# The gate weights as the stationary operand for four transposed tiles at once, and the put-off batches' columns cut into four parts

## The chip, the core and the metric

The program runs on one core of a Trainium2 chip. The metric is the time of one execution on the device in microseconds (us). The kernel before takes 1412.26 us (median of 3 runs, 1411.99 to 1412.28).

TensorE is PE in the profile (PEld is its weight load), VectorE is DVE, ScalarE is ACT, GpSimd is POOL, and SyncE, which issues most DMAs, is SP. A matmul has a stationary operand (the weights, loaded first) and a moving operand whose columns stream past it.

## The reference

Three stages follow each other, all in float32. Two attention steps give x, one row of 512 for each of 4608 tokens (8 batches of 576). A dense layer pair with a leaky ReLU follows: 512 to 2048 to 512. Then each token goes to one of 8 experts, which are chosen by the largest remaining of all logits, with at most 576 tokens for an expert.

```python
p_packed = sm_attn(p, k, v)
out = sm_attn(q, p_packed, p_packed)       # -> x [4608, 512]
h = x @ w_in
g = np.maximum(0.01 * h, h)
x2 = g @ w_out                             # [4608, 512]
logits = x2 @ w_gate                       # [4608, 8]
order = np.argsort(-logits.flatten())      # greedy assignment, capacity 576
...
out[mask] = np.maximum(x2[mask] @ w1[e], 0.0) @ w2[e]
```

The gate product x2 @ w_gate has only 8 columns. It is kept in float32, since the order of the logits decides the routing.

## The kernel before

**Stages.** `packs` computes the packed keys and values and folds the first dense layer into them (0 to about 125 us of the trace). `tokens` goes through batches 0 to 5 in 16 units each (128 of the 2048 hidden columns are one unit): `mm1` (L917) makes the hidden rows of the unit in two halves of 288 tokens, ACT and DVE evacuate and split them into a high and a low float32r part (L927, L928, L939, L942), and the second layer (`mm2_list`, L1082) adds 12 or 15 matmuls per unit to the batch's sums, one unit later. Batches 6 and 7 are put off: their first layer is done as side units inside batches 4 and 5 (`SIDE`, `side_unit`), split and stored to DRAM (`put`, L1011), and their second layer fills the PE's waits in the routing stage (`PutOff`), for which `get` (L1018) loads the stored parts again. Then come the routing (a serial chain of 12 steps on DVE and PE), and the experts.

**Where the logits come from.** For batches 0 to 4 the finished rows are multiplied by w_gate. `evac` (L1023) copies each 128-row tile out of PSUM and queues two pieces with `times_gate` (L1056): `turn` transposes the tile in four 128x128 blocks (L1065) and ACT copies them to SBUF (L1067); `product` (L1069) multiplies them by the gate weights, with the transposed block (128x128) as the stationary and the 8 gate columns as the moving operand (L1072), and DVE copies 128x8 to the logits L (L1073). For batches 5 to 7 the rows are not ready in time, so the kernel multiplies w_out by w_gate first (`wog_pieces`, the same two pieces for each of 16 tiles of w_out, whose high and low parts POOL adds at L953) and takes the logits from the hidden rows: `logits` (L961) has the 32 columns of `wog` of one unit as stationary operand and the unit's tokens as moving operand, in four column groups of the array (outputs on PSUM partitions 0, 32, 64 and 96). The 512 main tokens are four parts of 128 (L979); the 64 tail tokens go behind the fourth part (L980), and in batch 5 the tail tokens of batch 4 behind the first (L983). DVE adds the parts to `lg` (L986), and `logits_of` (L990) transposes `lg` back after the last unit (L996, L997).

**What sets the order.** On PE the order of batches 1 to 5 is written out in `tokens`: before each unit up to `XS` = 3 pieces are taken, those of the next batch's queries first, then gate pieces from `tk.dots` and, where room is left, from `gates` (the w_out pieces). They are emitted one at a time between the parts of the unit by `small()`. The functions of a piece without `pe` (the POOL addition) go with the piece in front. On all other engines, on PE in batch 0, and in the last four side units after batch 5, a scheduler orders the instructions by its own timeline. The PSUM bank of the pieces is `x`, with one buffer, or `acc5` in even batches.

A float32 matmul that isn't a transpose appears in the trace as two records, a transpose as one: the 38 products of four matmuls are 304 records of L1072, and the 48 units of `logits` are 384 records of L979.

Of the kernel before, what the change touches and what calls it, by code (L numbers as in the profile page):

```python
# [6 lines left out]
F32 = mybir.dt.float32  # L7
# [9 lines left out]
B, H, S, DH, NP_ = 8, 8, 576, 64, 32  # L17
D, FF = 512, 2048
E, F2, CAP = 8, 1024, 576
# [9 lines left out]
class Lag:  # L29


    def __init__(self):
        self.q = []
# [29 lines left out]
def pe(fn):  # L63

    def piece():
        return fn()
    piece.pe = True
    return piece
# [14 lines left out]
def f32(ap):  # L83
    return ap.bitcast(F32)
# [421 lines left out]
QE, XS = 14, 3  # L506
# [10 lines left out]
ND = 2  # L517
# [261 lines left out]
class Tokens:  # L779
# [165 lines left out]
    def wog_pieces(self):  # L945

        nc = self.nc
        st = {}

        def whole(f):  # L950
            t = self.two.tile([128, D], F32, name="wsum", tag="raw64")
            st[f] = t
            nc.gpsimd.tensor_add(t, f32(self.wo(f, 0)), f32(self.wo(f, 1)))  # L953

        fns = []
        for f in range(self.NF):
            turn, product = self.times_gate(lambda f=f: st[f], lambda f=f: self.wog[:, f, :E])
            fns += [lambda f=f: whole(f), turn, product]
        return fns

    def logits(self, b, f, tf):  # L961

        nc, PE = self.nc, self.nc.tensor
        both = b == B - ND - 1
        if f == 0:
            if b < B - ND:
                t = self.P.two.tile([128, 192], F32, name="lg2", tag="at2")  # L970
            else:
                t = self.one.tile([128, 192], F32, name="lg")
            nc.gpsimd.memset(t, 0.0)
            self.lg[b] = t
        lg = self.lg[b]
        ps = self.bank([128, 192])
        w = self.wog[:, f]
# [12 lines left out]
    def logits_of(self, b):  # L990
        nc = self.nc
        V, PE = nc.vector, nc.tensor
        c0, c8 = 9 * (b // 2) + 4 * (b % 2), 9 * (b // 2) + 8
        lt = self.lg.pop(b)
        ps = self.P.ps.tile([128, 2, 4, 4 * E], F32, name="x")
        PE.transpose(ps[:, 0].rearrange("p q e -> p (q e)"), lt[:, :128], self.ident)  # L996
        PE.transpose(ps[:64, 1].rearrange("p q e -> p (q e)"), lt[:, 128:], self.ident)  # L997
        V.tensor_copy(self.L[:, c0:c0 + 4], ps[:, 0, :, :E])
        lo = (b % 2) * 64
        V.tensor_copy(self.L[lo:lo + 64, c8], ps[:64, 1, 3, :E])  # L1000
        if b == B - ND - 1:
            V.tensor_copy(self.L[:64, c8], ps[:64, 1, 0, :E])
        if b % 2:
            self.R.look(self.two, c0 - 4, c0 + 5)

# [17 lines left out]
    def evac(self, b, acc, gate=True):  # L1023

        nc, P = self.nc, self.P
        V, A = nc.vector, nc.scalar
        bp = b // 2
        for r in range(4):
# [3 lines left out]
            if gate:  # L1032
                self.gate(x, 9 * bp + 4 * (b % 2) + r)
        if b % 2:
            x = self.wk1.tile([128, D], F32, name="x2tail")
            A.copy(x, acc[4])
            for i in range(2):
                r0 = (b - 1 + i) * S + 512
                nc.sync.dma_start(self.x2d[r0:r0 + 64], x[64 * i:64 * i + 64])
            if gate:  # L1040
                self.gate(x, 9 * bp + 8)
                self.dots.add([lambda: self.R.look(self.two, 9 * bp, 9 * bp + 9)])

    def gate(self, x, col):

        self.dots.add(self.times_gate(lambda: x, lambda: self.L[:, col]))

    def bank(self, shape):

# [6 lines left out]
    def times_gate(self, rows, out):  # L1056

        nc, PE = self.nc, self.nc.tensor
        st = {}

        def turn():
            x = rows()
            ps = self.bank([128, 4, 128])
            for c in range(4):
                PE.transpose(ps[:, c], x[:, c * 128:(c + 1) * 128], self.ident)  # L1065
            st["t"] = self.two.tile([128, 4, 128], F32, name="rowt")
            nc.scalar.copy(st["t"], ps)  # L1067

        def product():  # L1069
            ps = self.bank([128, E])  # L1070
            for c in range(4):
                PE.matmul(ps, st["t"][:, c], self.wg[:, c], start=c == 0, stop=c == 3)  # L1072
            nc.vector.tensor_copy(out(), ps)  # L1073
        return [pe(turn), pe(product)]


def mm2_list(nc, acc, g, tl, wh, wl, start, stop):
# [343 lines left out]
def tokens(tk, pk, keep, first, st, acc_pools):  # L1421
# [43 lines left out]
    for b in range(B - ND):  # L1465
# [3 lines left out]
        for q in SIDE_Q[b]:  # L1469
            if q:  # L1470
                side_q(*q)
            elif b + 1 < B - ND:
                nat, fns = tk.q_side(b + 1)
                qs.add(fns)
        with ordered(tk.tc, b > 0):
            for f in range(NF):
# [3 lines left out]
                if f % 2 == 0:  # L1480
                    wcur = w
                    nb, nf = (b, f // 2 + 1) if f // 2 < 7 else (b + 1, 0)
                    if nb < B - ND:
# [4 lines left out]
                        w = tk.wp_load(nb, nf)  # L1488
                tk.spare = b > 0 and b % 2 == 0 and 2 <= f

                xs = must[:]
                must.clear()
                if b:
                    tabs.pop(1)
                    for x in (qs, tk.dots, gates):
# [3 lines left out]
                    for more in (tk.dots, gates):  # L1499
                        while len(xs) < XS:  # L1500
                            x = more.take()
                            if x is None:
                                break
                            xs.append(x)

                def small(n=1):
                    for _ in range(min(n, len(xs))):
# [2 lines left out]
                t = tk.mm1(at, wcur, slice((f % 2) * 128, (f % 2) * 128 + 128))  # L1510
# [129 lines left out]
```

## Time and profile before

| | |
|---|---|
| median of the runs | 1412.26 us |
| profiled execution: its own time | 1415.55 us |
| profiled execution: span of the core | 1413.8 us |
| PE busy | 1347.5 us, 95% of the span |
| PE weight load busy | 1126.1 us, 80% |
| DVE busy | 732.4 us, 52% |
| ACT busy | 559.5 us, 40% |
| POOL busy | 309.1 us, 22% |
| batches 1 to 5 with the side units | about 250 to 806 us |
| routing | about 830 to 960 us |

Busy time is the union of an engine's instructions. Matmuls are pipelined and overlap in the records, so what one costs is read from the start of one group to the start of the next, not from its duration. The time of the profiled execution is 3.3 us above the median, and its span 1.5 us.

### The profile page before, as it was taken

The page shows a single profiled execution, that of the slowest core. Times are in us where ns is not written, and L with a number is a line of the kernel's source. Part 1 is how long each engine was busy: PE and PEld are TensorE (multiplying, and loading weights), DVE is VectorE, ACT ScalarE, POOL GpSimd, SP SyncE. Part 2 cuts the span into 40 slices and gives each one's busy share as a digit, 9 for nine tenths or more (in the row PEclk, how much of TensorE's full clock was granted, in tenths as well). Part 3 has the DMA queues.
Part 4 walks back from the last instruction along what each step waited for, and adds up shares of the span by engine and source line. Part 5 has one row for each costly group of instructions (what it writes and reads, how often), then busy time and mean ns, then how long its engine had stood idle before and what let it go on. Part 6 is the DMA issues. An engine that isn't in the chain of part 4 may idle for free. (4 is left out here: it accounts for less than half of the span.)

```text
span 1413.8 us, 25670 instructions
## 1 busy us (share of the span) xinstructions
PE 1347.5 (95%) x10206; PEld 1126.1 (80%) x10206; DVE 732.4 (52%) x1878; ACT 559.5 (40%) x1209; POOL 309.1 (22%) x293
## 2 busy tenths in 40 slices
PE   7999898999999999999999988997999999999997
PEld 4667776888888888788788866776998998898896
DVE  4776898433354445666455566782344344344331
ACT  4765555544445345555444420003233233233231
POOL 3322234244222112322122110002121121121011
PEclk9999999999999999999999999997999999999999
DMA  9998565210212112333223464546243443442320
GB/s 267 305 300 259 183 193 167 84 32 20 85 41 75 51 40 77 126 111 107 103 97 110 139 211 136 158 129 220 94 134 102 137 135 93 146 134 77 117 76 38
DMA packets 147881, 180.49 MB, mean 128 GB/s; under 512 B 27952, under 2 KB 105776, under 8 KB 147760
## 3 DMA queue, kind: packets, MB, share of 16 engines
q1 hardware_dynamic: 122992, 141.08, 32.1%
q10 hardware_dynamic: 19008, 18.88, 4.6%
q0 software_dynamic: 5760, 18.88, 3.7%
q8 instruction: 81, 1.33, 0.4%
q14 instruction: 40, 0.33, 0.1%
HBM read 124.27 MB, written 54.53 MB: 126 GB/s over the span
## 5 line engine op out<-in xcount | busy, mean ns | idle before, releaser
L1082 PE MATMUL acc<-wout,g 128*128 128x512 f32 x1728 | 454.3, 407 | 15.3 <-ACT wout L803 5.7
L1082 PEld LDWEIGHTS acc<-wout,g 128*128 128x128 f32 x1728 | 315.0, 191 | 84.0 <-issue 7.5
L928 DVE SCALAR_TENSOR_TENSOR t<-t 128x576 f32<-128x576 f32 x128 | 105.1, 821 | 140.1 <-ACT t L927 139.7
L927 ACT COPY t<-h 128x288 f32<-128x288 f32 x256 | 100.9, 400 | 182.0 <-PE h L80 181.8
L78 PE MATMUL h<-xt,w1hl 128*128 128x288 f32 x504 | 149.1, 296 | 2.0 <-DVE eg__12337 L1216 2.0
L79 PE MATMUL h<-xt,w1hl 128*128 128x288 f32 x504 | 149.3, 296 | 0.0
L80 PE MATMUL h<-xt,w1hl 128*128 128x288 f32 x504 | 149.2, 296 | 0.0
L78 PE MATMUL h<-at,wphl 128*128 128x288 f32 x384 | 123.7, 322 | 0.6 <-ACT t L927 0.6
L79 PE MATMUL h<-at,wphl 128*128 128x288 f32 x384 | 114.0, 297 | 0.0
L80 PE MATMUL h<-at,wphl 128*128 128x288 f32 x384 | 113.7, 297 | 0.0
L905 POOL TENSOR_TENSOR wphl<-wpraw,wphl 128x512 fp32r<-128x512 f32 x48 | 68.2, 1420 | 190.2 <-ACT wphl L904 189.4
L942 DVE TENSOR_TENSOR g<-t,g 128x512 fp32r<-128x512 f32 (+1 forms) x96 | 80.8, 841 | 39.7 <-ACT g L939 39.4
L78 PEld LDWEIGHTS h<-xt,w1hl 128*128 128x128 f32 x504 | 95.3, 189 | 4.8 <-ACT w2hl L1107 2.4
L1158 POOL DMA_INDIRECT xg<-x2d,idx x36 | 34.6, 960 | 288.6 <-PE x L1181 148.6
L79 PEld LDWEIGHTS h<-xt,w1hl 128*128 128x128 f32 x504 | 95.3, 189 | 2.4
L80 PEld LDWEIGHTS h<-xt,w1hl 128*128 128x128 f32 x504 | 95.3, 189 | 0.0
L78 PEld LDWEIGHTS h<-at,wphl 128*128 128x128 f32 x384 | 73.0, 190 | 14.1 <-issue 7.9
L1221 POOL DMA_INDIRECT out_dram<-ot,idx x32 | 43.9, 1371 | 171.5 <-DVE ot L1234 163.9
L939 ACT CAST g<-t 128x512 fp32r<-128x512 f32 (+1 forms) x96 | 64.8, 675 | 40.1 <-DVE t L928 38.2
L79 PEld LDWEIGHTS h<-at,wphl 128*128 128x128 f32 x384 | 73.1, 190 | 0.8
L80 PEld LDWEIGHTS h<-at,wphl 128*128 128x128 f32 x384 | 72.7, 190 | 0.1
L1108 DVE TENSOR_TENSOR w2hl<-w2raw,w2hl 128x1024 fp32r<-128x1024 f32 x31 | 38.0, 1225 | 59.0 <-ACT w2hl L1107 58.7
(790 smaller groups left out, 2407.2 us busy)
## 6 DMA issues: line engine op xcount, KB each, us to landing
gd<-g SPq DMA_DIRECT2D x32, 576.0 KB, 3.3
wp<-ev ACTq DMA_DIRECT2D x64, 256.0 KB, 4.5
w1raw<-in_moe_w_dram SPq DMA_DIRECT2D x30, 512.0 KB, 4.0
w2raw<-in_moe_w_dram SPq DMA_DIRECT2D x30, 512.0 KB, 3.6
wpraw<-wp SPq DMA_DIRECT2D x48, 256.0 KB, 2.7
g<-gd SPq DMA_DIRECT2D x16, 576.0 KB, 4.2
rawk<-in_k_dram SPq DMA_DIRECT2D x16, 512.0 KB, 6.6
rawv<-in_v_dram SPq DMA_DIRECT2D x16, 512.0 KB, 7.1
```

The costliest lines, as they stand in the source:

```text
L78: nc.tensor.matmul(ps, lh, rh, start=first and i == 0, stop=False)
L79: nc.tensor.matmul(ps, lh, rl, start=False, stop=False)
L80: nc.tensor.matmul(ps, ll, rh, start=False, stop=last and i == n - 1)
L905: nc.gpsimd.tensor_sub(w[:, 1], t, f32(w[:, 0]))
L927: A.copy(t[:, 64 + hf * HS:64 + (hf + 1) * HS], ps)
L928: V.scalar_tensor_tensor(t[:, 64:], t[:, 64:], 0.01, t[:, 64:], op0=OP.mult, op1=OP.max)
L939: A.copy(g[:, 0, c0:], tf[:, c0:])
L942: V.tensor_sub(g[:, 1, c0:], tf[:, c0:], f32(g[:, 0, c0:]))
L1082: mms.append(lambda: nc.tensor.matmul(acc[i], lhs, rhs, **kw))
L1108: sub(w[:, 1], t, f32(w[:, 0]))
L1158: self.nc.gpsimd.indirect_dma_start(out=t, out_offset=None, in_=self.x2d[:], in_offset=self.off(qb))
L1221: st = self.nc.gpsimd.indirect_dma_start(out=self.out, out_offset=self.off(qb), in_=t, in_offset=None)
```

## The change

The gate weights `wg` are widened to 32 columns with zeros behind the 8 (a memset on POOL, and the load into the first 8). `times_gate` takes a list of tiles. For four tiles it gives four `turn` pieces, which write one buffer, then a piece `products` and a piece `flip`. In `products` the 32 gate columns are the stationary and the transposed blocks the moving operand: 16 matmuls of 128 columns, the four tiles in the four column groups, with c outermost. DVE copies the 128x128 result to SBUF, `flip` transposes it in one matmul, and DVE copies out 8 columns of each group. The tail tile of batches 1 and 3 keeps the old `product`. The w_out pieces are made in groups of four as well, and they go in front of the same queue `tk.dots` instead of one of their own.

In `logits` the tail tokens are spread over the four column groups: 160, 160, 128 and 128 columns in batches 6 and 7, four times 160 in batch 5. There are four matmuls in place of five or six, and two DVE additions in place of two (one in place of three in batch 5). Since the parts no longer lie on 128-token borders, `logits_of` brings them back with 7 or 10 matmuls of 32, 64 or 128 stationary columns against 32 columns of the identity, instead of two transposes.

```diff
-        self.wg = P.one.tile([128, 4, E], F32, name="wg")
-        self.nc.sync.dma_start(self.wg, w_gate.rearrange("(c p) e -> p c e", p=128))
+        self.wg = P.one.tile([128, 4, 4 * E], F32, name="wg")
+        self.nc.gpsimd.memset(self.wg, 0.0)
+        self.nc.sync.dma_start(self.wg[:, :, :E], w_gate.rearrange("(c p) e -> p c e", p=128))
...
-        for f in range(self.NF):
-            turn, product = self.times_gate(lambda f=f: st[f], lambda f=f: self.wog[:, f, :E])
-            fns += [lambda f=f: whole(f), turn, product]
+        for f in range(0, self.NF, 4):
+            *turns, product, flip = self.times_gate([lambda f=f + i: st[f] for i in range(4)], lambda f=f: self.wog[:, f:f + 4, :E])
+            for i in range(4):
+                fns += [lambda f=f + i: whole(f), turns[i]]
+            fns += [product, flip]
...
         for q in range(4):
-            PE.matmul(ps[32 * q:32 * q + 32, :128], w, tf[:, 128 + 128 * q:256 + 128 * q], start=True, stop=q in (1, 2) or q == 0 and not both)
-        PE.matmul(ps[96:, 128:], w, tf[:, 64:128], start=False, stop=True)
-        tails = [slice(96, 128)]
-        if both:
-            PE.matmul(ps[:32, 128:], w, self.kept[:, f], start=False, stop=True)
-            tails.append(slice(0, 32))
-        for o in [(slice(0, 128), slice(0, 128))] + [(x, slice(128, 192)) for x in tails]:
+            PE.matmul(ps[32 * q:32 * q + 32, :cuts[q + 1] - cuts[q]], self.wog[:, f], tf[:, cuts[q]:cuts[q + 1]], start=True, stop=True)
+        for o in [(slice(0, 128), slice(0, 160))] if cuts[0] == 0 else [(slice(0, 128), slice(0, 128)), (slice(0, 64), slice(128, 160))]:
             nc.vector.tensor_add(lg[o], lg[o], ps[o])
+    def cuts(self, b):
+        return (0, 160, 320, 480, 640) if b == B - ND - 1 else (64, 224, 384, 512, 640)
...
-        PE.transpose(ps[:, 0].rearrange("p q e -> p (q e)"), lt[:, :128], self.ident)
-        PE.transpose(ps[:64, 1].rearrange("p q e -> p (q e)"), lt[:, 128:], self.ident)
+        for k, c, n, p in [(r, 128 + 128 * r, 128, 0) for r in range(4)] + [(4, cuts[0], 128 - cuts[0], lo)]:
+            while n:
+                q = max(i for i in range(4) if cuts[i] <= c)
+                m = max(x for x in (32, 64, 128) if p % x == 0 and x <= min(n, cuts[q + 1] - c))
+                l = c - cuts[q]
+                PE.matmul(ps[p:p + m, k], lt[:, l:l + m], self.ident[:, 32 * q:32 * q + 32], start=True, stop=True)
+                c, n, p = c + m, n - m, p + m
...
-            st["t"] = self.two.tile([128, 4, 128], F32, name="rowt")
-            nc.scalar.copy(st["t"], ps)
+            if i == 0:
+                t = self.two.tile([128, 4, 4, 128], F32, name="rowt", bufs=1)
+                st["t"] = t
+            nc.scalar.copy(st["t"][:, i], ps)
...
+        def products():
+            ps = self.bank([128, 128])
+            for c in range(4):
+                for i in range(4):
+                    PE.matmul(ps[32 * i:32 * i + 32], self.wg[:, c], st["t"][:, i, c], start=c == 0, stop=c == 3)
+            t = self.two.tile([128, 128], F32, name="gates", bufs=1)
+            st["s"] = t
+            nc.vector.tensor_copy(t, ps)
+        def flip():
+            ps = self.bank([128, 4, 4 * E])
+            PE.transpose(ps.rearrange("p i e -> p (i e)"), st["s"], self.ident)
+            nc.vector.tensor_copy(out(), ps[:, :, :E])
...
-    qs, tabs, gates = Pieces(), Lag(), Pieces()
-    gates.add(tk.wog_pieces())
+    qs, tabs = Pieces(), Lag()
+    tk.dots.add(tk.wog_pieces())
```

On PE in batch 1, units 1 and 2 (`row` and `wsum` are tiles to be multiplied by the gate, `g` the hidden rows of L1082, `rawtail` a piece of the queries), the order before is this:

```order
L1065 MATMUL x<-ident,row 128x128 x4
L1082 MATMUL acc<-wout_88,g 128x512 x7
L1072 MATMUL x<-wg,rowt 128x8 x4
L1082 MATMUL acc<-wout_88,g 128x512
L1082 MATMUL acc_3271<-wout_88,g 128x512 x2
L1082 MATMUL acc<-wout_88,g 128x512 x4
L1082 MATMUL acc_3271<-wout_88,g 128x512
L578 MATMUL x<-ident,rawtail 128x64 x2
```

Here a unit holds the `turn` and the `product` of one tile. In the changed kernel, two units of two turns each are followed by a unit with the product of four tiles and the flip (L1084 is `products`, L1091 `flip`, L1101 the old L1082):

```order
L1084 MATMUL x<-rowt,wg 32x128 x16
L1101 MATMUL acc<-wout_88,g 128x512 x7
L1091 MATMUL x<-ident,gates 128x128
L1101 MATMUL acc<-wout_88,g 128x512
L1101 MATMUL acc_3274<-wout_88,g 128x512 x2
L1101 MATMUL acc<-wout_88,g 128x512 x4
L1101 MATMUL acc_3274<-wout_88,g 128x512
L842 MATMUL x<-kt,cpp 64x288 x2
```

Between `products` and `flip` stand seven matmuls of the second layer (six in the batches with 12 per unit). On PE at the end of batch 6's logits, before:

```order
L1082 MATMUL acc_7517<-wout_88,g 128x512
L979 MATMUL x<-t_7574,wog 32x128 x4
L980 MATMUL x<-t_7574,wog 32x64
L996 MATMUL x<-ident,lg 128x128
L997 MATMUL x<-ident,lg 64x128
L78 MATMUL h_7628<-at_6188,wphl 128x288
```

The same place in the changed kernel (L978 is `logits`, L1002 the matmuls of `logits_of`):

```order
L1101 MATMUL acc_7464<-wout_88,g 128x512
L978 MATMUL x<-t_7516,wog 32x160 x2
L978 MATMUL x<-t_7516,wog 32x128 x2
L1002 MATMUL x<-ident,lg 64x32
L1002 MATMUL x<-ident,lg 32x32 x2
L1002 MATMUL x<-ident,lg 128x32 x3
L1002 MATMUL x<-ident,lg 64x32
L78 MATMUL h_7574<-at_6154,wphl 128x288
```

Two transposes became seven matmuls. On SP, where the last side units store (`gd<-g`) and the put-off batches load (`g<-gd`), before:

```order
L1105 DMA w2raw<-in_moe_w_dram 128x2x512
L1018 DMA g<-gd 128x2x512
L1011 DMA gd<-g 256x1x576 x3
L1018 DMA g<-gd 128x2x512 x13
L1018 DMA g<-gd 128x2x576
```

And in the changed kernel:

```order
L1124 DMA w2raw<-in_moe_w_dram 128x2x512
L1022 DMA g<-gd 128x2x512
L1015 DMA gd<-g 256x1x576 x2
L1022 DMA g<-gd 128x2x512
L1015 DMA gd<-g 256x1x576
L1022 DMA g<-gd 128x2x512 x12
```

One load has moved in front of the last store.

## Rows read from the trace of the kernel before

**Rows 1.** Busy time by stage: window, length, engines' busy us (instructions), clock, DMA.
```profile
125.00:250.00 125.00, 109.54 (x575) 90.07 (x574) 106.40 (x421) 68.53 (x176) 39.73 (x41) 0.96 0.61 184
250.00:806.00 556.00, 550.99 (x3580) 463.34 (x3578) 270.43 (x488) 262.24 (x601) 137.68 (x112) 1.00 0.23 77
806.00:830.00 24.00, 16.50 (x113) 12.74 (x110) 14.17 (x51) 9.90 (x23) 8.04 (x12) 0.99 0.85 302
```

**Rows 2.** Waits of PE from 250 to 800 us: total, times, longest.
```profile
PE acc L979 <- DVE t L928: 3.0, 3, 1.2
```

**Rows 3.** Timeline of PE in batch 2: start, us from first start to last end.
```profile
408.04 2.96 PE L1082 MATMUL acc<-wout,g 128*128 128x512 f32 x12
410.93 0.71 PE L841 MATMUL x<-kt,cpp 128*64 128x288 f32 x4
...
413.27 2.96 PE L1082 MATMUL acc<-wout,g 128*128 128x512 f32 x12
416.07 0.60 PE L572 MATMUL x<-ident,rows 128*128 128x128 f32 x4
```

**Rows 4.** Timeline of PE, one unit of batch 3 with a turn and a product.
```profile
471.61 0.60 PE L1065 MATMUL x<-ident,row 128*128 128x128 f32 x4
471.96 1.86 PE L1082 MATMUL acc<-wout,g 128*128 128x512 f32 x7
473.67 0.95 PE L1072 MATMUL x<-wg,rowt 128*128 128x8 f32 x8
474.48 2.11 PE L1082 MATMUL acc<-wout,g 128*128 128x512 f32 x8
476.43 0.60 PE L572 MATMUL x<-ident,rows 128*128 128x128 f32 x4
```

**Rows 5.** Groups by line and shape, PE, 250 to 806 us: busy, mean ns | idle before.
```profile
L1072 PE MATMUL x<-wg,rowt 128*128 128x8 f32 x224 | 26.8, 246 | 0.0
...
L1072 PE MATMUL acc<-wg,rowt 128*128 128x8 f32 x80 | 9.5, 246 | 0.0
```

**Rows 6.** Timeline of PE and PEld in the first stage: float32 in four column groups.
```profile
23.07 0.49 PEld L764 LDWEIGHTS x<-rawv,at 128*32 128x32 f32 x32
23.07 0.65 PE L764 MATMUL x<-rawv,at 128*32 128x64 f32 x32
...
23.65 0.15 PEld L766 LDWEIGHTS x<-rawtailv,at 64*32 64x32 f32 x8
```

**Rows 7.** Timeline of PE around two units of logits in batch 5.
```profile
709.00 0.43 PE L979 MATMUL x<-t,wog 128*32 128x128 f32 x8
709.27 0.28 PE L980 MATMUL x<-t,wog 128*32 128x64 f32 x2
709.47 0.40 PE L78 MATMUL h<-at,wphl 128*128 128x288 f32 x1
...
711.25 0.43 PE L979 MATMUL x<-t,wog 128*32 128x128 f32 x8
...
711.72 1.90 PE L1082 MATMUL acc<-wout,g 128*128 128x512 f32 x7
713.45 0.61 PE L1065 MATMUL x<-ident,row 128*128 128x128 f32 x4
```

**Rows 8.** Timeline of PE at the end of batch 6's logits.
```profile
686.22 0.30 PE L996 MATMUL x<-ident,lg 128*128 128x128 f32 x1 [0.98 <-DVE lg L986]
686.36 0.27 PE L997 MATMUL x<-ident,lg 128*64 128x128 f32 x1
686.39 0.38 PE L78 MATMUL h<-at,wphl 128*128 128x288 f32 x1
```

**Rows 9.** Waits of PE from 800 to 832 us.
```profile
PE acc L1082 <- DMA g<-gd: 5.1, 3, 4.4
PE x L979 <- DVE lg L986: 1.9, 2, 1.1
```

**Rows 10.** Timeline of SP from 800 to 832 us.
```profile
816.31 7.66 SPq L1011 DMA_DIRECT2D gd<-g  x3
824.17 3.41 SPq L1018 DMA_DIRECT2D g<-gd  x3
```

**Rows 11.** Groups by line, POOL, 100 to 360 us: busy, mean ns | idle before, releaser.
```profile
L953 POOL TENSOR_TENSOR wsum<-wout 128x512 f32<-128x512 f32 x16 | 25.4, 1586 | 36.3 <-PE x L1065 36.1
```

More of the change, by code (lines that the diff above doesn't have):

```diff
@@ L966, in logits @@
         nc, PE = self.nc, self.nc.tensor
-        both = b == B - ND - 1
+        cuts = self.cuts(b)
         if f == 0:
             if b < B - ND:
-                t = self.P.two.tile([128, 192], F32, name="lg2", tag="at2")
+                t = self.P.two.tile([128, 160], F32, name="lg2", tag="at2")
             else:
-                t = self.one.tile([128, 192], F32, name="lg")
+                t = self.one.tile([128, 160], F32, name="lg")
             nc.gpsimd.memset(t, 0.0)
@@ L975, in logits @@
         lg = self.lg[b]
-        ps = self.bank([128, 192])
-        w = self.wog[:, f]
+        ps = self.bank([128, 160])
         for q in range(4):
-            PE.matmul(ps[32 * q:32 * q + 32, :128], w, tf[:, 128 + 128 * q:256 + 128 * q], start=True, stop=q in (1, 2) or q == 0 and not both)
-        PE.matmul(ps[96:, 128:], w, tf[:, 64:128], start=False, stop=True)
-        tails = [slice(96, 128)]
-        if both:
-            PE.matmul(ps[:32, 128:], w, self.kept[:, f], start=False, stop=True)
-            tails.append(slice(0, 32))
-        for o in [(slice(0, 128), slice(0, 128))] + [(x, slice(128, 192)) for x in tails]:
+            PE.matmul(ps[32 * q:32 * q + 32, :cuts[q + 1] - cuts[q]], self.wog[:, f], tf[:, cuts[q]:cuts[q + 1]], start=True, stop=True)
+        for o in [(slice(0, 128), slice(0, 160))] if cuts[0] == 0 else [(slice(0, 128), slice(0, 128)), (slice(0, 64), slice(128, 160))]:
             nc.vector.tensor_add(lg[o], lg[o], ps[o])
@@ L993, in logits_of @@
         c0, c8 = 9 * (b // 2) + 4 * (b % 2), 9 * (b // 2) + 8
-        lt = self.lg.pop(b)
-        ps = self.P.ps.tile([128, 2, 4, 4 * E], F32, name="x")
-        PE.transpose(ps[:, 0].rearrange("p q e -> p (q e)"), lt[:, :128], self.ident)
-        PE.transpose(ps[:64, 1].rearrange("p q e -> p (q e)"), lt[:, 128:], self.ident)
[L998 to L1002, printed above, removed]
+        lt, cuts = self.lg.pop(b), self.cuts(b)
+        both = cuts[0] == 0
+        lo = 0 if both else (b % 2) * 64
+        ps = self.P.ps.tile([128, 5, 4 * E], F32, name="x")
+        for k, c, n, p in [(r, 128 + 128 * r, 128, 0) for r in range(4)] + [(4, cuts[0], 128 - cuts[0], lo)]:
[5 more added lines that the diff above has]
+                c, n, p = c + m, n - m, p + m
+        V.tensor_copy(self.L[:, c0:c0 + 4], ps[:, :4, :E])
+        ts = slice(lo, lo + 128 - cuts[0])
+        V.tensor_copy(self.L[ts, c8], ps[ts, 4, :E])
         if b % 2:
@@ L1027, in evac @@
         bp = b // 2
+        rows = []
         for r in range(4):
@@ L1031, in evac @@
             nc.sync.dma_start(self.x2d[b * S:b * S + 512].rearrange("(p r) d -> r p d", r=4)[r], x)
-            if gate:
-                self.gate(x, 9 * bp + 4 * (b % 2) + r)
+            rows.append(x)
+        if gate:
+            c = 9 * bp + 4 * (b % 2)
+            self.dots.add(self.times_gate([lambda x=x: x for x in rows], lambda: self.L[:, c:c + 4]))
         if b % 2:
@@ L1040, in evac @@
             if gate:
-                self.gate(x, 9 * bp + 8)
+                self.dots.add(self.times_gate([lambda: x], lambda: self.L[:, 9 * bp + 8]))
                 self.dots.add([lambda: self.R.look(self.two, 9 * bp, 9 * bp + 9)])
-    def gate(self, x, col):
-        self.dots.add(self.times_gate(lambda: x, lambda: self.L[:, col]))
     def bank(self, shape):
@@ L1059, in times_gate, with turn @@
         st = {}
-        def turn():
-            x = rows()
+        def turn(i):
+            x = rows[i]()
             ps = self.bank([128, 4, 128])
@@ L1071, in product @@
             for c in range(4):
-                PE.matmul(ps, st["t"][:, c], self.wg[:, c], start=c == 0, stop=c == 3)
+                PE.matmul(ps, st["t"][:, 0, c], self.wg[:, c, :E], start=c == 0, stop=c == 3)
             nc.vector.tensor_copy(out(), ps)
-        return [pe(turn), pe(product)]
+        def products():
[10 more added lines that the diff above has]
+            nc.vector.tensor_copy(out(), ps[:, :, :E])
+        return [pe(lambda i=i: turn(i)) for i in range(len(rows))] + ([pe(product)] if len(rows) == 1 else [pe(products), pe(flip)])
 def mm2_list(nc, acc, g, tl, wh, wl, start, stop):
@@ L1494, in tokens @@
                     tabs.pop(1)
-                    for x in (qs, tk.dots, gates):
+                    for x in (qs, tk.dots):
                         x.lead()
@@ L1498, in tokens @@
                     xs += [x for x in (qs.take() for _ in range(-(-left // max(1, QE - f)))) if x]
[L1499 to L1504, printed above, removed]
+                    while len(xs) < XS:
+                        x = tk.dots.take()
+                        if x is None:
+                            break
+                        xs.append(x)
                 def small(n=1):
```

## The prediction

> **What bounds the kernel now.** I read the busy time by stage first. From 250 to 806 us, where batches 1 to 5 and the side units run, PE is busy for 550.99 of 556.00 us, while DVE has 270.43 and ACT 262.24 [rows 1]. The clock there is 1.00, the 2.4 GHz level. Second, the waits of PE in that stage: the largest group is 3.0 us in three waits, none over 1.2 us [rows 2]. So nothing else holds this stage: what PE no longer has to issue there moves the end, until another wait appears. All the products and all but four of the 48 units of logits lie in it. Third, the timeline of PE, for the price of each piece, from start to start.
>
> A plain matmul of the second layer: twelve start at 413.27 and the next group at 416.07, 2.80 us or 0.2333 each [rows 3]. Before a group in column groups of 64 the same twelve take 2.89 (408.04 to 410.93), so entering column groups costs 0.09 [rows 3]. After a product, eight take 1.95 (474.48 to 476.43) for 8 x 0.2333 = 1.87, so 0.08 is paid after it [rows 4]; behind a product nothing is paid ahead: the seven before it take 1.71 for 1.63, which is the same 0.08 after the turn [rows 4]. After column groups seven take 1.73 (711.72 to 713.45) for 1.63, so 0.10 is paid there [rows 7].
>
> **The products.** One takes 0.81 us (473.67 to 474.48) and 0.08 behind it, 0.89 [rows 4]. The trace has 224 + 80 = 304 records of 8 [rows 5], so 38 products; the two tail tiles keep theirs. Removed: 36 x 0.89 = 32.1 us. The moving operand is only 8 columns; what the engine does in those 0.81 us is to load a 128x128 stationary eight times, 0.10 each.
>
> Added are 9 times `products` and `flip`. Sixteen float32 matmuls are 32 records, in four column groups 8 rounds of 128 columns. The trace has such a thing with 64 columns: eight rounds, with accumulation, from 23.07 to 23.65 [rows 6]. 0.58 us less some 0.09 for leaving are 0.061 per round, so 0.122 for 128 columns. The other row is the logits: two rounds of 128 columns from 709.00 to 709.27, 0.135 each with their start in it [rows 7]. Bounds: 0.122 and 0.145 (0.58 / 8 doubled). I take 0.122, since rows 6 accumulate over rounds as this does. Leaving: the two rounds of 64 columns behind take 0.20 (709.27 to 709.47), so 0.20 - 0.12 = 0.08 [rows 7]. One `products`: 0.09 + 8 x 0.122 + 0.08 + 0.10 = 1.25 us, 11.2 for nine (12.9 by the upper bound). One `flip` is a transpose, 0.09 (four take 0.35, 471.61 to 471.96) to 0.14 (686.22 to 686.36), and 0.08 behind it [rows 4, 8]: 0.2, 1.8 for nine. The 38 turns stay. Sum: -32.1 + 11.2 + 1.8 = -19.1 us, between -17.4 and -20.
>
> The Trainium skill has a rule against this: by "TensorE: Matmul & The Clock Gate", Part 3, The mechanism, a weight load overlaps running matmuls only where it goes to other row groups, and here all four column groups use all rows. By rows 6 it does overlap: 32 loads and 32 matmuls end together, in 0.58 us, so the trace does not bear the rule out. It is the third rival below.
>
> **The logits.** A unit takes 0.47 us from its start to the next group, with one tail (709.00 to 709.47) and with two (711.25 to 711.72) [rows 7]: the two tails already ran side by side. New are two rounds of 160 columns, 0.27 x 160 / 128 = 0.34, and 0.08 for leaving: 0.42. That saves 0.05 per unit, 2.4 us over 48. With the round of rows 6 it would be 0.085, 4.1 us; at worst nothing. I take 2.4, from the row that has the same operands.
>
> **logits_of.** Two transposes cost 0.17 (686.22 to 686.39) and 0.08 behind [rows 8]. In their place come 14 records (batches 6 and 7) and 20 (batch 5), with changes between groups of 32, 64 and 128 columns, of a form that the trace does not have. Lower bound: as dense as rows 6, 0.58 / 32 = 0.018 each, and 0.27 to enter and leave: 0.5 and 0.6. Upper bound: 0.10 each as in the old product [rows 4], four more changes of 0.09: 2.1 and 2.7. So each call costs 0.3 to 2.4 us more. I take 0.10 for the 128-column stationaries, as in rows 4, and 0.02 for the small ones: about 1 us each. The one of batch 7 lies beside a wait of PE for a load that lasts 4.4 us [rows 9], so it counts nothing; batch 5's lies in the same waiting stretch, half counted; batch 6's counts in full. Sum +1.6 (0.5 to 5).
>
> By the skill's "TensorEngine Tiling (Array Packing)", Instruction Overhead, a small matmul costs some 60 cycles (0.025 us at the full clock) whatever its columns; with that the three calls would cost about 0.5 us each. The trace's nearest 128-column rows have 0.10.
>
> **The new wait.** `flip` needs DVE's copy of the product, and seven (or six) matmuls of 1.4 to 1.6 us stand between on PE. On DVE that copy stands right behind L928 in most units, but in batches 2 to 4 also behind softmax work of the queries. Behind the waiting `flip` on PE stand the other half of the unit's second layer and the next `mm1`, and DVE and ACT wait for that. The longest wait of PE on DVE now is 1.2 us [rows 2]. Bounds: 0, and 9 x 1.2 = 10.8. The four to five units that have a full softmax decide it; I take +1.0. The buffer of the turned tiles is single, but the next `turn` follows the products in PE's own order, so that costs nothing.
>
> **Order that the scheduler makes.** In batch 0 the POOL additions of L953 have moved: three of them now stand between the subtractions that finish w_out at the end of batch 0, 1.59 us each [rows 11], in a stretch where PE has some 15 us of idle time in 125 [rows 1]. The PE order there differs in many places too. Bounds -4 and +5; I take +1.0. At the end, SP's fourth load `g<-gd` stands before the last store instead of behind it. The three stores hold SP from 816.31, and the load after them starts at 824.17 [rows 10], for which PE waits 4.4 us [rows 9]. The load can come at most the last store's share earlier, some 2.9 us. Against that stands its own buffer, which must be free. I take -1.5 (0 to -2.9). The memset and the later load of `wg` lie before the first PE work: nothing.
>
> **The sum.** -19.1 - 2.4 + 1.6 + 1.0 + 1.0 - 1.5 = -19.4 us. Against the profiled execution: its own time 1415.55 becomes 1396.2, its span 1413.8 becomes 1394.4. The median lies 3.3 us below that execution's time; I put the same difference on it: 1412.26 - 19.4 = 1392.9 us. A difference under 0.2%, 2.8 us, is what the measurement can't tell from none.
>
> **The rivals.**
>
> 1. The wait of `flip` eats half of the gain: 9 x 1.2 = 10.8 in place of 1.0, 1402.7 us. For it: the DVE order in batches 2 to 4. Against it: DVE is half idle in the stage [rows 1].
> 2. The order of batch 0 and a dear `logits_of` take back what their bounds allow: 4 + 3.4 more, 1400.3 us. For it: POOL's additions stand ahead of subtractions that PE needs. Against it: PE, DVE and ACT wait for one another there already, and what is late in one chain is often early in the next.
> 3. Weight loads are not hidden in column groups: 0.10 per round [rows 4] in 8 rounds of nine products, 7.2 us, 1400.1. It is the skill's rule of above. Against it: rows 6.
> 4. The other side: the four column groups take turns once they add into one bank with 128 columns each. Then `products` is 32 rounds, 32 x 0.122 + 0.27 = 4.2 us, with `flip` 4.4, against 4 x 0.89 = 3.6 removed: +0.8 x 9 = +7 in place of -19.1, and the rest of the sum is -0.3: about 1419 us, slower. It decides from the point where the rounds take over three times as long as in rows 6. For it: nothing shows accumulation with 128 columns. Against it: rows 6 accumulate with 64, and rows 7 run 128 columns side by side.
>
> **Chances.** The forecast, 1385 to 1398 us: 0.73. Rival 1: 0.08. Rival 2: 0.09. Rival 3: 0.03. Rival 4: 0.04. The rest, 0.03, is something that no row shows, half of it near no change. The range that leaves out two in ten at most: 1384 to 1403, with rivals 1 to 3 at its upper end and, at its lower, -20 for the products, -4.1 for the logits, -2.9 and -4 for the order, with +1 for `logits_of`: about -30 would be 1382, cut to what is likely. Faster by over 0.2%: 0.93; within 0.2%: 0.02; slower: 0.05.
>
> **What would show it.** Right: the records of `products` are 288, and one of them takes 1.0 to 1.2 us from its first start to the next group; batches 1 to 5 end some 21 us earlier, near 786; PE stays over 98% busy there; the wait of `flip` for DVE is under 3 us in total. Wrong: a list of PE waits with `flip` and DVE at the top (rival 1); starts of the four column groups 0.1 us apart instead of under 0.01 (rival 4); rounds of 0.2 us or more (rival 3); a later start of batch 1 than 250 us by several us (rival 2).

## The result and the profile after

The changed kernel takes 1399.6 us (median of 4 runs, 1397.24 to 1401.9), against 1412.26 us before: ratio 0.9903, 95% interval 0.9887 to 0.9919. It is faster by 12.7 us by the medians. The forecast was 1392.9 us with a range of 1384 to 1403. So the direction and the range hold, but a third of the forecast gain (19.4 us) is missing, and the time lies outside the likeliest case's own range of 1385 to 1398 us, next to rivals 2 and 3 (1400.3 and 1400.1). The profiled execution took 1398.82 us, its span is 1397.1 us.

The busy time by stage (window, length, then busy us of PE, PEld, DVE, ACT and POOL, granted clock, DMA share, GB/s) answers to [rows 1]:

```profile
125.00:250.00 125.00, 108.46 (x566) 89.11 (x560) 105.66 (x411) 66.04 (x168) 39.05 (x40) 0.95 0.60 178
250.00:787.00 537.00, 528.17 (x3431) 428.37 (x3431) 262.65 (x445) 261.78 (x600) 141.25 (x114) 0.99 0.24 79
787.00:810.00 23.00, 20.22 (x150) 15.57 (x148) 10.21 (x28) 10.51 (x22) 5.97 (x5) 1.00 0.75 254
```

The long stage ends at 787 us instead of 806, as was forecast (786). But PE was idle for 5 us in it before and is for 9 us now. Where, the list of PE's waits from 250 to 787 us says (what waits, for what; total us, times, longest), which answers to [rows 2]:

```profile
PE acc L1101 <- POOL wout L807: 3.6, 2, 2.7
PE acc L978 <- DVE t L929: 2.4, 3, 1.1
PE acc L1101 <- ACT wout L804: 1.0, 1, 1.0
PE x L1002 <- DVE lg L980: 1.0, 1, 1.0
PE x L1084 <- ACT rowt L1072: 0.7, 1, 0.7
```

The wait of `flip` for DVE, the first rival, isn't in the list at all. At its top stand waits of the second layer for w_out, which were not there: they belong to the end of batch 0.

The prices came out as forecast. The timeline of PE in batch 1 (start, us, line, form, count) has one `products` and its `flip`; the last two lines are one unit of batch 6's logits, which stands in batch 4. They answer to [rows 4, 7]:

```profile
274.14 0.29 PE L80 MATMUL h<-at,wphl 128*128 128x288 f32 x1
274.36 1.08 PE L1084 MATMUL x<-rowt,wg 128*32 128x128 f32 x32
275.37 1.89 PE L1101 MATMUL acc<-wout,g 128*128 128x512 f32 x7
277.10 0.27 PE L1091 MATMUL x<-ident,gates 128*128 128x128 f32 x1
277.13 1.18 PE L1101 MATMUL acc<-wout,g 128*128 128x512 f32 x4
...
567.52 0.47 PE L978 MATMUL acc<-t,wog 128*32 128x160 f32 x8
567.92 0.40 PE L78 MATMUL h<-at,wphl 128*128 128x288 f32 x1
```

`products` takes 1.01 us (274.36 to 275.37), with 0.09 ahead (274.14 to 274.36 is 0.22, an L80 alone 0.13) and 0.10 behind (seven matmuls in 1.73 instead of 1.63): 1.20, forecast 1.25. `flip` takes 0.03, and about 0.08 behind it: 0.11, forecast 0.2. A unit of logits takes 0.40 (0.41 in batch 5), forecast 0.42, before 0.47.

The price that was wrong stands between the two. POOL's timeline at the end of batch 0, before (the part that answers is its last subtraction for w_out, L806):

```profile
237.40 1.42 POOL L806 TENSOR_TENSOR wout<-w,wout 128x256 fp32r<-128x256 f32 x2 [2.77 <-ACT wout L803]
...
250.58 1.19 POOL L806 TENSOR_TENSOR wout<-w,wout 128x256 fp32r<-128x256 f32 x1
251.83 0.53 POOL L897 MEMSET wog<- 128x512 f32 x1
```

The first line is the 27th of the 32 subtractions, the line with 250.58 the last. After the change (the subtractions are now L807), the 27th starts at 243.32 and the last at 258.67, with POOL's additions (L954) between:

```profile
243.32 1.22 POOL L807 TENSOR_TENSOR wout<-w,wout 128x256 fp32r<-128x256 f32 x1 [4.26 <-ACT wout L804]
244.50 2.89 POOL L954 TENSOR_TENSOR wsum<-wout 128x512 f32<-128x512 f32 x2
247.36 0.91 POOL L807 TENSOR_TENSOR wout<-w,wout 128x256 fp32r<-128x256 f32 x1
...
256.93 1.78 POOL L954 TENSOR_TENSOR wsum<-wout 128x512 f32<-128x512 f32 x1
258.67 1.31 POOL L807 TENSOR_TENSOR wout<-w,wout 128x256 fp32r<-128x256 f32 x1
```

The last part of w_out is 8.1 us later. PE empties, and then its clock falls. By windows of 5 us, before (where the clock had its drop earlier, and PE is full from 250 us on):

```profile
245.00:250.00 5.00, 4.30 (x12) 3.44 (x13) 2.94 (x6) 3.92 (x11) 2.31 (x3) 0.66 0.41 107
255.00:260.00 5.00, 5.00 (x32) 4.36 (x31) 0.76 (x1) 4.67 (x11) 1.84 (x2) 1.00 0.70 198
```

and after:

```profile
250.00:255.00 5.00, 4.11 (x22) 3.01 (x22) 4.94 (x9) 2.85 (x9) 3.21 (x3) 1.00 0.57 169
255.00:260.00 5.00, 1.32 (x5) 0.53 (x3) 3.26 (x6) 2.56 (x6) 3.73 (x3) 0.91 0.01 2
260.00:265.00 5.00, 4.97 (x14) 4.02 (x15) 0.00 (x0) 0.88 (x2) 1.97 (x3) 0.50 0.00 0
265.00:270.00 5.00, 5.00 (x31) 4.34 (x30) 0.76 (x1) 4.74 (x11) 2.50 (x2) 0.91 0.80 241
```

PE is busy for 1.32 of 5 us, and after that pause the clock is at its lower level (0.50, 1.2 GHz) for 5 us in which PE has a full load. This is the sign that the forecast had set for its second rival, a later start of batch 1. Note also that the 27th subtraction is already 5.9 us late, ahead of the first of these additions.

### The profile page after: what moved, and what is told of

The parts are those of the page before. It is cut to its first block, busy times and chain, and to the rows that moved or that the text cites. A ratio compares the mean times of both kernels' runs of the same rounds, so it can differ in the third digit from the quotient of the medians.

```text
span 1397.1 us, 25466 instructions
## 1 busy us (share of the span) xinstructions
PE 1330.5 (95%) x10129; PEld 1095.0 (78%) x10129; DVE 723.8 (52%) x1827; ACT 560.5 (40%) x1209; POOL 310.9 (22%) x294
## 5 line engine op out<-in xcount | busy, mean ns | idle before, releaser
L1101 PE MATMUL acc<-wout,g 128*128 128x512 f32 x1728 | 453.8, 408 | 12.2 <-DMA g<-gd 4.1
L1101 PEld LDWEIGHTS acc<-wout,g 128*128 128x128 f32 x1728 | 315.8, 191 | 90.3 <-issue 12.0
L80 PE MATMUL h<-xt,w1hl 128*128 128x288 f32 x504 | 148.5, 295 | 0.0
L80 PE MATMUL h<-at,wphl 128*128 128x288 f32 x384 | 114.2, 298 | 0.6 <-POOL wphl L906 0.6
L80 PEld LDWEIGHTS h<-xt,w1hl 128*128 128x128 f32 x504 | 94.6, 188 | 0.0
L78 PEld LDWEIGHTS h<-at,wphl 128*128 128x128 f32 x384 | 72.9, 190 | 24.1 <-issue 14.6
L80 PEld LDWEIGHTS h<-at,wphl 128*128 128x128 f32 x384 | 73.1, 191 | 0.8 <-POOL wphl L906 0.8
```

The source lines that it names most:

```text
L78: nc.tensor.matmul(ps, lh, rh, start=first and i == 0, stop=False)
L80: nc.tensor.matmul(ps, ll, rh, start=False, stop=last and i == n - 1)
L1101: mms.append(lambda: nc.tensor.matmul(acc[i], lhs, rhs, **kw))
```

## The experiments

All times are compared by the ratio to the kernel before, measured beside each group of runs, since its median was not the same each time (1412.26, 1414.03, 1414.37, 1414.82 us).

| kernel | median us | ratio (95%) | against before, us |
|---|---|---|---|
| changed kernel | 1399.6 | 0.9903 (0.9887 to 0.9919) | -13.7 |
| e10: buffers in m1 | 1386.87 | 0.981 (0.9794 to 0.9826) | -26.9 |
| e9: before, larger m2 | 1422.64 | 1.0067 (1.0053 to 1.0082) | +9.5 |
| e2: changed, old logits | 1406.65 | 0.9951 (0.9938 to 0.9965) | -6.9 |
| e4: before, new logits | 1410.14 | 0.9974 (0.9963 to 0.9985) | -3.7 |
| e14: additions late | 1399.25 | 0.9883 (0.9861 to 0.9906) | -16.5 |
| e12: m1, groups in series | 1399.01 | 0.9882 (0.9859 to 0.9904) | -16.7 |
| e13: m1, old logits | 1397.76 | 0.9878 (0.9856 to 0.9901) | -17.3 |
| e11: m1, rows first | 1389.2 | 0.9807 (0.9785 to 0.983) | -27.3 |
| e15_pad86 | 1404.47 | 0.9923 (0.9909 to 0.9936) | -10.9 |
| e16: old logits, 42 pads | 1397.67 | 0.9885 (0.987 to 0.99) | -16.3 |
| e15_pad32 | 1392.33 | 0.9839 (0.9826 to 0.9853) | -22.8 |

The last column is (ratio - 1) times the median of before that was measured with the run.

**Why batch 0 ends late.** The forecast saw the new order but named no cause for it. Of the change, the queue, in which the w_out pieces now come first, could be one. But the change also makes the pool `m2` larger: `rowt` is one buffer of four tiles (8 KB a partition) instead of two of one tile (4 KB). e10 takes the two buffers from another pool:

```diff
-                t = self.two.tile([128, 4, 4, 128], F32, name="rowt", bufs=1)
+                t = self.one.tile([128, 4, 4, 128], F32, name="rowt")
-            t = self.two.tile([128, 128], F32, name="gates", bufs=1)
+            t = self.one.tile([128, 128], F32, name="gates")
```

> The changed kernel with the two buffers of the turned tiles and of the gate product taken from another pool (m1), so that the pool m2 does not grow; in its compiled order DVE's work of batch 0 stands as in the kernel before, and the first two additions of w_out's parts stand early again. Theory A (the order of batch 0 took the rest of the gain; it comes from the size of the pool): the last part of w_out is ready near 252 us instead of 260, the first unit of batch 1 no longer waits 3.6 + 1.0 us, the clock does not fall to 0.50 at 260; about 1393 us (1391 to 1396) and runs that agree within 1 us. Theory B (the order of batch 0 is a wash; the profiled execution of before was simply long): 1399.6 +- 1.5 us. Theory C (the taking back of the logits by many small matmuls ate it): 1399.6 +- 1.5 us as well.

e9 is the counterpart in the kernel before, with nothing of the change but the room:

```diff
-            st["t"] = self.two.tile([128, 4, 128], F32, name="rowt")
+            st["t"] = self.two.tile([128, 4, 128], F32, name="rowt", bufs=4)
```

> The kernel before with four buffers of the turned tile instead of two, so that its pool m2 is as large as in the changed kernel; no work is added, and DVE's order in batch 0 is then that of the changed kernel. Theory A: last part of w_out at about 258 to 260 us, PE waits 4 to 8 us more there; 1412.3 + 6 = about 1418 us (1415 to 1421). Theories B and C: 1412.3 +- 1 us.

Both bear out theory A, and by more than it said: e10 gains 12.7 us on the changed kernel by the medians (13.2 by the ratios), and e9, whose queues are those of the kernel before, loses 9.5 us with no work added. (That the runs of e10 would agree within 1 us did not come true: 1384.19 to 1388.07.) The order goes with the room as well. Of the 426 DVE instructions that the kernel before runs between 125 and 260 us, 423 stand in the same order in e10, but only 319 in the changed kernel and 318 in e9; and of the changed kernel's 181 ACT instructions there all stand in the same order in e9, 125 in the kernel before. So ACT has another order too, not DVE alone. In e10, the same windows:

```profile
250.00:255.00 5.00, 4.99 (x32) 4.30 (x31) 1.41 (x2) 4.90 (x12) 3.76 (x3) 1.00 0.65 186
255.00:260.00 5.00, 5.00 (x37) 4.00 (x39) 0.97 (x1) 1.98 (x6) 3.92 (x3) 1.00 0.62 190
260.00:265.00 5.00, 5.00 (x52) 3.65 (x44) 1.98 (x4) 1.07 (x2) 0.00 (x0) 1.00 0.03 9
```

PE does not stop, the clock stays at 1.00, and the last subtraction starts at 246.80 us. Unit 6 of batch 1 starts 14.5 us earlier than in the changed kernel, and this difference stays between 14.3 and 14.6 us until the side units end. Summed over PE's records from 119 us to that unit, nearly the same work takes 181 us in the changed kernel and 167 in e10: idle time 21.6 against 15.6 us, and 159.2 against 151.4 us from start to start of the matmuls. The granted clock of this stretch is 0.94 in the changed kernel and 0.99 in e10, so more than half of the price is the clock. The forecast for it had only waits. Why the larger pool makes the scheduler order the engines otherwise (by the size itself or by the addresses that move with it) no run separates; that stays open.

e14 asks for the mechanism in the forecast's second rival, that POOL's additions stand ahead of subtractions. It gives the sums another pool, whose room comes free only at the end of batch 0:

```diff
-            t = self.two.tile([128, D], F32, name="wsum", tag="raw64")
+            t = self.one.tile([128, D], F32, name="wsum", bufs=2)
```

> The changed kernel with the tile of the added w_out parts (wsum) taken from pool m1, whose room becomes free only at the end of batch 0: POOL's three additions then stand behind its last subtraction of w_out; DVE's order and PE's are as in the changed kernel, with the large pool m2. Theory P (the prediction's rival 2 as it was put: POOL's additions ahead of the subtractions make w_out late, and slow DVE beside them, where steps of 0.42 us take up to 1.5): most of the 12.7 us between the changed kernel and the one with the small m2 comes back, about 1389 to 1393 us. Theory D (it is the order of DVE's steps since 170 us, by which w_out's last parts are already 5 to 9 us late before the first addition): 2 to 4 us come back, about 1396 to 1399 us.

Theory D is borne out, theory P is not: 2.8 us come back by the ratio (0.4 by the medians, so the times alone can hardly tell it from nothing), and 3.4 us at unit 6 of batch 1 in the trace, where the last subtraction starts at 254.52 us, 4.2 earlier than in the changed kernel. So the additions cost some 3 us, and the other ten lie in the rest of the order. No run changed DVE's order alone.

e11 puts the pieces for w_out behind the rows, with the buffers in m1:

```diff
-    tk.dots.add(tk.wog_pieces())
...
+                    if (b, f) == (1, 1):
+                        tk.dots.add(tk.wog_pieces())
```

> The changed kernel with the buffers in m1, and the pieces for w_out behind the rows of batch 0 in the one queue instead of ahead of them (put in at unit 1 of batch 1). Theory: which of the two comes first changes nothing while PE waits for neither: 1386.9 +- 1.5 us. Rival: POOL's additions in batch 1, three for each unit, still stand ahead of others and cost: 1383 to 1385 us.

The ratio is 0.9807 against 0.981, though the median is 2.3 us higher: these runs can tell no difference. Where the pool is small, the order of the two kinds of pieces shows no price.

**The products.** e12 turns the two loops in `products`:

```diff
-            for c in range(4):
-                for i in range(4):
+            for i in range(4):
+                for c in range(4):
```

> The changed kernel with the buffers in m1 (1386.9 us), and in the products the loop over the four tiles outermost: the same 16 matmuls, but four after each other go to one column group, so that neighbours no longer lie in different groups. Theory S (the four groups run side by side only where neighbouring matmuls lie in different groups): a product is 32 passes of about 0.11 us, 3.5 us instead of 1.01, nine of them +22 us: about 1409 us (1404 to 1414). Rival: what matters is only that the stationary operand is small, so its loads are hidden in either order: 1386.9 +- 2 us.

It is 12.1 us slower than e10 by the medians, 10.2 by the ratios, and its side units end 12.7 us later. The timeline of PE in e12 has the product at 2.39 us:

```profile
261.73 2.46 PE L1084 MATMUL x<-rowt,wg 128*32 128x128 f32 x32
264.12 1.20 PE L1101 MATMUL acc<-wout,g 128*128 128x512 f32 x4
```

and in e10 at 1.01:

```profile
280.23 1.08 PE L1084 MATMUL x<-rowt,wg 128*32 128x128 f32 x32
281.24 1.90 PE L1101 MATMUL acc<-wout,g 128*128 128x512 f32 x7
```

Nine times 1.38 us is 12.4. So the side-by-side groups are what pays, and the rival falls. Theory S's size was too high, since even then part of the passes overlap: of the 32 starts some follow at 0.109 us and some in pairs. With 2.39 us the change would still gain, 0.89 x 4 = 3.6 us being removed for each; the fourth rival needed more than three times the round, and this is the nearest that a run came to it.

**The logits.** e2 and e4 separate the two parts in the kernels as they were, e13 with the buffers in m1. In each the functions `logits` and `logits_of` of one kernel stand in the other:

```diff
-            PE.matmul(ps[32 * q:32 * q + 32, :cuts[q + 1] - cuts[q]], self.wog[:, f], tf[:, cuts[q]:cuts[q + 1]], start=True, stop=True)
...
+            PE.matmul(ps[32 * q:32 * q + 32, :128], w, tf[:, 128 + 128 * q:256 + 128 * q], start=True, stop=q in (1, 2) or q == 0 and not both)
+        PE.matmul(ps[96:, 128:], w, tf[:, 64:128], start=False, stop=True)
...
```

> The changed kernel with the logits and their taking back as before (128 columns in four groups with the tails behind, two transposes); only the products are new. By the prediction the logits' part is worth -2.4 + 1.6 = -0.8 us, so this is about 1400.4 us. Theory C: the part is a loss of 4 us or more, so this is 1396 us or less. Theory A: 1400.4 +- 2 us, with the same late w_out and the same scatter of runs (over 2 us).

> The kernel before with only the logits' part new (160 columns in four groups, 7 to 10 small matmuls to take them back). The order of batch 0 is that of before. Prediction: 48 units save about 0.075 us each by the changed kernel's own trace (3.6 us), the taking back costs 3 x 0.3 to 1.4 more, of which one lies beside a wait: 1411.5 us (1409 to 1413). Theory C: 1416 us or more.

> The changed kernel with the buffers in m1, and the logits and their taking back as before: only the products are new, and the order of batch 0 is as before. With the logits' part worth 3.9 us (measured in the kernel before): 1386.9 + 3.9 = about 1391 us (1389 to 1393), which leaves 23 us for the products against the 19.1 - 1.0 = 18.1 of the prediction. If the two parts need each other (the logits' part was worth 5 us or more in the large m2): 1392 to 1395 us.

Theory C falls: the part gains. But what it gains is 3.7 us in the kernel before, 6.8 in the changed one (-13.7 against -6.9) and 9.6 with the buffers in m1 (-26.9 against -17.3), where 0.8 was forecast and its own matmuls save 48 x 0.07 = 3.4 us, of which the calls that take the logits back cost some 1.2 each again. So e2 (1406.65) and e13 (1397.76) lie above all that was expected of them. The milestones of the traces show where this lies (us):

| | before | changed | e10 | e13 | e15_pad86 | e16 |
|---|---|---|---|---|---|---|
| first layer of the side units ends | 814.42 | 806.10 | 791.75 | 791.90 | 805.95 | 796.85 |
| first counting matmul (L343) | 838.85 | 828.64 | 816.24 | 817.71 | 827.40 | 824.22 |
| last one ends | 941.71 | 927.65 | 916.00 | 925.19 | 934.58 | 926.70 |
| the routing between these two | 102.86 | 99.01 | 99.76 | 107.48 | 107.18 | 102.48 |
| PE's idle time in it | 5.99 | 3.70 | 4.32 | 8.53 | 7.94 | 5.36 |
| granted clock in it | 0.98 | 1.00 | 1.00 | 0.95 | 0.95 | 0.98 |

e10 and e13 reach the end of the side units within 0.15 us of each other. The old logits lose 1.3 us in the tail and 7.7 in the routing, a stage that the change does not touch. The other pair has it too: 107.01 us in e2 against 99.01 in the changed kernel, and 102.86 before against 99.74 in e4. There PE stands still where nothing in the trace releases it. e13 in the routing:

```profile
856.39 1.45 PE L343 MATMUL cnt<-cmp,oh 128*32 128x64 bf16 x136
861.38 0.30 PE L343 MATMUL cnt<-cmp,oh 128*32 128x64 bf16 x8 [3.54 <-issue]
```

and e10:

```profile
842.35 1.46 PE L343 MATMUL cnt<-cmp,oh 128*32 128x64 bf16 x141
846.14 0.21 PE L343 MATMUL cnt<-cmp,oh 128*32 128x64 bf16 x3 [2.32 <-issue]
```

Of these 7.7 us, 4.2 are idle time of PE. The other 3.5 go with the clock, which falls behind the pause; e13 again, by a window:

```profile
860.00:865.00 5.00, 3.62 (x16) 2.53 (x17) 1.61 (x10) 0.00 (x0) 0.00 (x0) 0.50 0.03 5
```

Where the pauses fall goes with the number of records ahead of them. Counted over all records of PE and PEld, the pauses of over 0.6 us between the first and the last L343 end at record 63, 63 and 61 modulo 256 in before, 63, 63, 61 in e13, 65 and 65 in e10, 69 and 69 in the changed kernel. Each of the 16 pauses of over 1.9 us that the routing has in all traces together overlaps a transfer of a DMA queue of kind "instruction": in e13 one from 859.00 to 859.96, within the pause from 857.83 to 861.38. That queue makes 80 transfers in e10, for 20,258 records of PE and PEld, one for 253. That PE waits there for the next piece of its own code, at a border in its program, fits these numbers; no run shows it directly. The new logits need 172 records fewer ahead of the routing, so the borders fall elsewhere in its steps. The last three runs move them by transposes that nobody reads:

```diff
+                if (b, f) == (B - ND - 1, 8):
+                    ps = tk.bank([128, 4, 128])
+                    for i in range(86):
+                        nc.tensor.transpose(ps[:, i % 4], tk.ident, tk.ident)
```

> The changed kernel with the buffers in m1 (1386.9 us), and 86 transposes of the identity that nobody reads, on PE in unit 8 of batch 5. In the traces so far PE's unexplained pauses in the routing all stand at PE record 61 to 69 modulo 256, and with the old logits the first counting matmul of the routing (L343) is record 10942 = 190 modulo 256, with the new ones 10770 = 18. Theory F (the logits' part gained 7 of its 9.6 us only because PE's program is shorter by 172 records, by which the pauses at the borders fall elsewhere): 86 x 2 records bring the border back to 190, so the routing (first to last L343) is about 107 us instead of 99.8: 1386.9 + 86 x 0.09 + 7.5 = about 1402 us. Rival G (the routing is shorter because of what the logits' part does itself): routing 99.8 +- 1 us, 1386.9 + 7.7 = about 1394.6 us.

> The other way round: products new, logits as before, buffers in m1 (1397.8 us), and 42 such transposes, which bring L343's first record from 190 to 190 + 84 = 274 = 18 modulo 256. Theory F: the routing falls from 107.5 to about 99.8 us, and added work makes the kernel faster: 1397.8 + 3.8 - 7.7 = about 1394 us. Rival G: routing 107.5 +- 1 us, 1397.8 + 3.8 = about 1401.6 us.

> The changed kernel with the buffers in m1 and 32 such transposes: L343's first record at 82 modulo 256, a place that no run has had. Theory F: the routing differs from 99.8 us by what its borders cost there, anything between 98 and 107 us, with pauses at record 61 to 69 modulo 256 again, and the time is 1386.9 + 2.9 + that difference: 1388 to 1397 us. Rival G: routing 99.8 +- 1 us, 1389.8 us.

e15_pad86 decides against rival G: with the new logits and the border at e13's place, the routing takes 107.18 us, like e13's 107.48, with the long pause again inside the counting matmuls:

```profile
870.54 0.30 PE L343 MATMUL cnt<-cmp,oh 128*32 128x64 bf16 x7 [3.61 <-issue]
```

The time, 1404.47, is 17.6 us above e10 where theory F had 15.2 (the 86 transposes take 9.6 us, 0.112 each, where 7.7 was expected). e16 shows the converse, but only in part: its routing falls from 107.48 to 102.48 us, 5.0 of the 7.7 expected, and the 42 transposes cost 5.0 in the stage and 1.5 more in the tail, so that the time is what it was (1397.67 against 1397.76) instead of 3.8 less. Rival G's time, 1401.6, is as far off, and its routing of 107.5 further than F's 99.8. e15_pad32 lies in F's range with a routing of 103.66 us. It is not the time by which the routing is later: e12 begins it 15.2 us after e10 with the same records ahead, and its routing takes 99.82 us. But the place of the border isn't all: of six runs with the border at e10's place, four (the changed kernel, e10, e11, e12) have a routing of 99.0 to 99.9 us at a granted clock of 1.00, and two (e14 and e16) have 102.04 and 102.48 at 0.98. Why the clock fell in these two, and what decides how much of a border's pause a step shows, stays open.

## Why the prediction was right, and where not

**Products: right.** Forecast -19.1; by the prices above it is the 32.1 removed less 9 x (1.20 + 0.11) = 11.8 added, so -20.3. e13, with the products alone, is 17.3 us faster although its routing is 4.6 us longer than before's.

The reading that carried it is that of [rows 6]: four column groups with 64 columns and accumulation took 0.061 a round, so 128 columns would take 0.122. They took 1.01 / 8 = 0.126 with the leaving in it; a round starts every 0.109 us. The third and fourth rivals fall with that. One reading of [rows 6] was not exact: loads and matmuls don't end together, the loads end at 23.56 us and the matmuls at 23.72. That they overlap stands.

**Logits: right in kind, too small.** A unit saves 0.07 instead of 0.05 us: 3.4 instead of 2.4.

**logits_of: right.** Batch 6's call takes 1.41 us against 0.17 for its two transposes [rows 8], so 1.2 more, where about 1 was taken. Its passes with a 128-column stationary start 0.11 apart, as those of [rows 4] do (0.10). In the changed kernel's timeline of PE:

```profile
676.61 1.48 PE L1002 MATMUL x<-ident,lg 128*64 128x32 f32 x14 [0.97 <-DVE lg L980]
678.02 0.40 PE L78 MATMUL h<-at,wphl 128*128 128x288 f32 x1
```

Batch 5's call, with 20 records, takes no longer: 1.20 us (798.09 to 799.29); 16 of its records have 32 or 64 columns and start in pairs 0.007 apart.

**The wait of `flip`: right on the safe side.** +1.0 was taken, none is there.

**The order at the end: about right, but not sure.** -1.5 was taken; PE's longest wait for the load fell from 4.4 us [rows 9] to 3.3. The stretch from the end of the side units to the routing fell from 24.4 to 22.5 us, but e10, with the same change, has 24.5. Of SP's stores [rows 10] only the last now stands between two loads, in the changed kernel:

```profile
PE acc L1101 <- DMA g<-gd: 3.3, 1, 3.3
```

```profile
813.79 0.57 SPq L1022 DMA_DIRECT2D g<-gd  x1
814.45 0.57 SPq L1015 DMA_DIRECT2D gd<-g  x1
816.28 10.64 SPq L1022 DMA_DIRECT2D g<-gd  x4
```

**The order of batch 0: the step that failed.** "Bounds -4 and +5; I take +1.0": it was 9.5 us in the kernel before and 13 in the changed one. The second rival named the place, a late w_out at the end of batch 0, and the sign, but made POOL's additions the cause, which is 3 us of it. The bound of +5 had no term for the clock: the 6.0 us of idle time are near that bound, but another 7.8 us came with the lower clock. And that the single buffer of the turned tiles "costs nothing" looked at waits for the buffer, not at the room it takes.

**Not in the sum at all: the routing**, 102.86 to 99.01 us, 3.9 us of the gain in the profiled executions. So the time lies in the forecast's range in part by luck: two errors partly cancel, +12 for batch 0 and -4 for the routing, and some -3 come from terms that came out a little better than forecast.

e10 is the faster version: 1386.87 us, the changed kernel with its two buffers in m1, ratio 0.981 (0.9794 to 0.9826).

## What to carry to other kernels

A buffer's size is part of a change's price where a scheduler orders the rest: give the old kernel the new room first and compare the orders; here the room was worth 13 us. A pause of PE can cost more than its own length, so the granted clock behind it has to be read too. A product with few columns was cheapest here as four column groups with the narrow operand stationary and neighbouring matmuls in different groups (1.01 us, against 2.39 with neighbours in one group and 4 x 0.89 with the wide operand stationary).

## What the runs showed of the hardware

**Pauses that go with the count of PE's records.** A serial stage's length depended on how many PE records stand ahead of it: 86 transposes in an earlier stage changed the routing from 99.76 to 107.18 us, of which 3.6 are idle time of PE and the rest goes with a granted clock of 0.95 instead of 1.00.

**DVE beside POOL.** In the changed kernel's timeline of DVE, the steps of w_out's reading slow down while POOL adds (244.50 to 247.39):

```profile
242.38 0.42 DVE L110 SCALAR_TENSOR_TENSOR w<-raw,w 128x256 f32<-128x256 f32 x1
242.72 0.42 DVE L105 SCALAR_TENSOR_TENSOR w<-raw,w 128x256 int32<-128x256 int32 x1
...
244.75 1.51 DVE L110 SCALAR_TENSOR_TENSOR w<-raw,w 128x256 f32<-128x256 f32 x1
246.18 1.50 DVE L105 SCALAR_TENSOR_TENSOR w<-raw,w 128x256 int32<-128x256 int32 x1
...
248.80 0.42 DVE L110 SCALAR_TENSOR_TENSOR w<-raw,w 128x256 f32<-128x256 f32 x1
```

A step of 0.42 us takes 1.5 us, about as long as one addition (1.45). By the Trainium skill, "SBUF — State Buffer", section Who interferes with whom, a DVE instruction with two SBUF inputs contends with a GpSimd instruction that reads SBUF, and the port pair that they share is an exclusive lock. The trace agrees: 1.51 and 1.50 against 0.42 us. This may be a part of the 3 us that the additions cost in e14, beside their own time on POOL; no run separates the two.
